# Column totals, spread of norms and transposition of three batches: from TensorE to VectorE's 32x32 blocks and DRAM

## Chip, cores and metric

The kernel runs on one core of a Trainium2 chip. The metric is the device time of one execution in microseconds. A core has five engines that work in parallel, each on its own list of instructions in order: PE (TensorE, matmuls, with PEld for its weight loads), DVE (VectorE), ACT (ScalarE), POOL (GpSimd) and SP (SyncE, which here issues the DMA transfers). Times of three runs before: 2155.27 us at the median, 2154.85 to 2155.99.

## What is computed

Channel attention for four batches, followed by a gated layer for all tokens. Cut to what matters:

```python
# q, k, v: (4, 6080, 256) float32; w_in (256, 2048), w_out (2048, 256)
qn = q / (norm(q, axis=1) + 1e-6)          # one norm per column, over 6080 rows
kn = k / (norm(k, axis=1) + 1e-6)
s  = kn.transpose(0, 2, 1) @ qn / tau      # 256 x 256 per batch
a  = softmax(s)
x  = (v @ a).reshape(24320, 256)
h  = x @ w_in
g  = h * sigmoid(1.702 * h)
out = g @ w_out
```

The weights come in and leave as 64-bit words of which the kernel uses 32-bit floats. Every large product is made of three products of high and low parts.

## The kernel before

**The main loop.** The product `v @ a @ w_in` is made as `v @ (a @ w_in)`: for each batch the 256x256 attention is folded into the input weights, and the main loop multiplies `v` by the folded weights. A step of the main loop is a *pair*: one batch, one chunk of tokens (six in a batch, of twice 512 tokens, one of twice 480) and two blocks of the hidden layer, eight pairs to a chunk. A pair issues 45 matmuls: 21 of `product` (line 800, seven products by a seven-product scheme in three terms, into the PSUM banks `ps_x`, `ps_y`, `ps_z`) and 24 of `project` (line 876, into `ps_o`). Between them stand ACT's copies and gates (`copied` line 834, `seed` 839, `gate` 854, `high` 859) and DVE's sums and low parts (`add` 843, which makes `r` from `ps_x`, and `low` 863, which makes `gl`). Results leave by `out_T` (line 891), issued by SP through three `osb` buffers.

**The side work.** While batch b is being multiplied, the attention of batch b + 1 is prepared in the gaps of the other engines: loads of q and k, their high and low parts, scores (`score_half`, line 388, gathered by `collect`, 406), and squares for the norms (ACT squares, POOL adds into `acc`, a tile of 128 partitions by 256 columns for q and for k). The rest is one chain per batch:

- `norms_sum` (415): four matmuls of `acc` with a column of ones give the sum over partitions of each column, `ps_n`; in float32 each matmul is two passes. `norms_copy` (424), `norms_root` on POOL (427), `norms_b` (431 to 436: plus 1e-6, reciprocal, and `diag`, the identity scaled by the norms of q).
- `norms_spread` (441): two matmuls of ones with `diag` put the norms of q in every partition, `ps_b`; `norms_q` (448) copies them to `rq`.
- `softmax_a` (495, 499), `softmax_b` (504, the exponential), `softmax_c` (517).
- `transposes` (525): four passes of PE turn the 256x256 attention `x` over, into `ps_t`. `turned` and `turned_low` (534, 537) make its parts `aT_h`, `aT_l`; `mixed` (546 on ACT copies `ps_t` to `whole`, 556 on DVE makes four sums of its quarters), and `mixed_split` (563, 565) their parts.
- `fold_load` (575) brings parts of the input weights from DRAM, `fold` (592) multiplies, and `fold_take` (603 on ACT for a first copy, 606 on DVE for a sum) puts the block product into `wf`. POOL and ACT and DVE make the weights of the next batch of it.

**What sets the order.** Each engine's instructions are put in one list by a planner that is written in the kernel: a `Job` is a row of steps with an engine, a planned duration, what each needs, a due time and an earliest begin, both counted in pairs. The planner places the steps in the gaps that it expects. PE's side work goes only into three slots of a pair (`at=("S", None)` is one of them). `turn` gives the step that must be over before a buffer may be used again. The first batch has a start-up of its own, written out by hand.

Of the kernel before, what the change touches and what calls it, by code (L numbers as in the profile page):

```python
# [11 lines left out]
F32 = mybir.dt.float32  # L12
# [3 lines left out]
ALU = mybir.AluOpType  # L16
AX = mybir.AxisListType
# [11 lines left out]
def channel_attention_then_glu(  # L29
# [169 lines left out]
    class Attention:  # L199
# [210 lines left out]

        def norms_sum(self):
            self.ps = bank("s", "ps_n")
            for n in range(2 * NC2):
                acc, i = self.acc[:, n // NC2, :], n % NC2
                nc.tensor.matmul(  # L415
                    self.ps[:, n : n + 1],
                    lhsT=acc[:, i * P : (i + 1) * P],
                    rhs=ones[:, 0:1],
                    start=True, stop=True,
                )  # L420

        def norms_copy(self):
            self.rn = small.tile([P, 2 * NC2], F32, tag="rn", name="rn")
            nc.vector.tensor_copy(self.rn, self.ps[:, : 2 * NC2])
# [4 lines left out]
        def norms_b(self):  # L429
            rn = self.rn  # L430
            nc.vector.tensor_scalar_add(rn, rn, 1e-6)
            nc.vector.reciprocal(rn, rn)
            self.diag = sp.tile([P, NC2, P], F32, tag="sq", name="diag", bufs=2)
            for i in range(NC2):
                nc.vector.tensor_scalar_mul(self.diag[:, i, :], ident, rn[:, i : i + 1])
            nc.vector.tensor_scalar_mul(rn[:, NC2:], rn[:, NC2:], rtau)

        def norms_spread(self):
            self.ps = bank("s", "ps_b")
            for i in range(NC2):  # L440
# [100 lines left out]
        def mixed(self, n):  # L541
            if n == 0:
                both = sp.tile([P, 2, NC2 * C], F32, tag="qs", name="mixed")
                self.whole = both[:, 0].rearrange("p (c x) -> p c x", c=NC2)
                self.mix = both[:, 1].rearrange("p (n x) -> p n x", n=4)
                nc.scalar.copy(self.whole, self.ps)
                return
# [7 lines left out]
            )[n - 1]  # L555
# [38 lines left out]
        def fold_take(self, s, k, n):  # L594
# [7 lines left out]
            if add is None:  # L602
                nc.scalar.copy(at[out], src)
# [863 lines left out]
    def weight_job(b, s, begin):  # L1467
# [9 lines left out]
        for k, (_, _, takes) in enumerate(FOLD):  # L1477
# [9 lines left out]
            for n, name in enumerate(names):  # L1487
                eng = "DVE" if k else "ACT"
                job.add(eng, 1.1, name, [(*key, k) if n == 0 else names[n - 1]], A.fold_take, s, k, n)
# [108 lines left out]
    def softmax_job(b, begin):  # L1598
        A = ats[b]
        job = Job(begin, begin)  # L1600
# [6 lines left out]
        last += [("sums", b, len(A.units))]  # L1607
        add("PE", 0.4, "sum", last, A.norms_sum, at=("S", None))
        add("DVE", 0.3, "copy", [(*key, "sum")], A.norms_copy)
        add("POOL", 1.0, "root", [(*key, "copy")], A.norms_root)  # L1610
        room = turn("sq", (*key, "b"), [(*key, "spread")])
        add("DVE", 2.4, "b", [(*key, "root"), *room], A.norms_b)
        add("PE", 0.6, "spread", [(*key, "b")], A.norms_spread, at=("S", None))
        room = turn("sq", (*key, "q"), [(*key, "x")])
        add("DVE", 0.6, "q", [(*key, "spread"), *room], A.norms_q)
        room = turn("qs", (*key, "x"), [(*key, "t")])
        add("DVE", 3.6, "x", [(*key, "q"), *room], A.softmax_a)
# [3 lines left out]
        add("PE", 0.7, "t", [(*key, "c")], A.transposes, at=("S", None))  # L1621
        add("ACT", 1.0, "turn", [(*key, "t")], A.turned)
        job.add("DVE", 1.15, ("turned", b), [(*key, "turn")], A.turned_low)
        room = turn("qs", (*key, ("mix", 0)), [("mixed", b)])
        add("ACT", 1.0, ("mix", 0), [("turned", b), *room], A.mixed, 0)
        for n in range(1, 5):
            add("DVE", 0.45, ("mix", n), [(*key, ("mix", n - 1))], A.mixed, n)
        used = [("fold", b, NG // 2 - 1, len(FOLD) - 2)]
        room = turn("sq", (*key, ("mix", "h")), used) + turn("sq", (*key, ("mix", "h")), used)
        add("ACT", 1.0, ("mix", "h"), [(*key, ("mix", 4)), *room], A.mixed_split, False)  # L1630
# [161 lines left out]
    for b in range(B):  # L1792
# [6 lines left out]
        if b + 1 < B:  # L1799
# [15 lines left out]
            softmax_job(b + 1, o + p + 1)  # L1815
# [44 lines left out]
```

## Time and profile before

| what | before |
|---|---|
| time, median of 3 runs | 2155.27 us (2154.85 to 2155.99) |
| time of the profiled execution | 2155.06 us |
| its span | 2153.1 us |
| mean granted clock of PE | 0.999 |
| busy PE / PEld / DVE / ACT / POOL | 100 / 83 / 61 / 72 / 20% |
| share of the chain that ended last: PE | 98% |
| matmuls on lines 876 (3 x 1536) and 800 (21 in each of 192 pairs) | 4608 and 4032 |
| share of the DMA engines used | 24% |

The span runs from the first to the last instruction that the profiler recorded; the 2 us that the execution takes longer lie around it. The records of matmuls overlap, so the busy share of PE is read with care: what a matmul takes of the stream is the distance between the starts of its neighbours. Idle time of the other engines costs nothing as long as PE doesn't wait for them.

### The profile page before, as it was taken

How to read it: one execution, taken by the hardware profiler on the slowest of the kernel's cores; microseconds unless marked ns; L12 is line 12 of the kernel's file. 1: busy time of each engine (PE TensorE's matmuls, PEld its weight loads, DVE VectorE, ACT ScalarE, POOL GpSimd, SP SyncE). 2: the span in 40 equal slices, each digit the busy share in tenths (PEclk: the TensorE clock that was granted, in tenths of full speed). 3: DMA queues.
4: the chain of work that ended last, by engine and by line, in shares of the span. 5: the costliest groups of instructions: out<-in, count | busy, mean ns of one | idle time of the engine just before them, and what ended most of it. 6: DMA issues, size and time to landing. Idle time of an engine off the chain costs nothing.

```text
span 2153.1 us, 26788 instructions
## 1 busy us (share of the span) xinstructions
PE 2144.7 (100%) x9702; PEld 1791.1 (83%) x9702; DVE 1321.3 (61%) x1990; ACT 1548.6 (72%) x2749; POOL 436.1 (20%) x465
## 2 busy tenths in 40 slices
PE   9999999999999999999999999999999999999999
PEld 8888888888888888888888888888888888888887
DVE  7986666665566666665566666666566555445543
ACT  7987777777667777776766777777676666666665
POOL 0003234330212323231021332332102110100100
PEclk9999999999999999999999999999999999999999
DMA  9433325221322222221122222132122110110100
GB/s 371 164 103 98 118 94 166 74 79 40 108 87 79 64 78 66 95 73 33 55 92 88 84 64 88 50 97 75 30 71 94 54 55 25 54 40 20 57 20 19
DMA packets 89397, 173.45 MB, mean 81 GB/s; under 512 B 8624, under 2 KB 16304, under 8 KB 89264
## 3 DMA queue, kind: packets, MB, share of 16 engines
q1 hardware_dynamic: 89264, 171.74, 24.0%
q8 instruction: 76, 1.25, 0.2%
q14 instruction: 57, 0.47, 0.1%
HBM read 136.32 MB, written 35.39 MB: 80 GB/s over the span
## 4 chain that ended last, share of the span: by engine, by line
PE 98%; ACT 1%; DMA 1%; DVE 0%; issue 0%; ACTq 0%; SPq 0%
PE ps_o L876 48%; PE ps_x L800 24%; PE ps_z L800 12%; PE ps_y L800 6%; PE s L388 4%; PE s L349 2%; PE ps_w L592 1%; DMA words<-in_w_in 1%; PE ps_w L645 0%; DMA words<-in_w_out 0%; PE ps_y L901 0%; ACT g L854 0%; ACT z L134 0%; DVE vl L782 0%; PE ps_n L415 0%
## 5 line engine op out<-in xcount | busy, mean ns | idle before, releaser
L876 PE MATMUL ps_o<-gh,wo_l 128*128 128x512 f32 (+1 forms) x1536 | 594.9, 387 | 0.0
L876 PE MATMUL ps_o<-gh,wo_h 128*128 128x512 f32 (+1 forms) x1536 | 594.8, 387 | 0.0
L876 PE MATMUL ps_o<-gl,wo_h 128*128 128x512 f32 (+1 forms) x1536 | 470.5, 387 | 0.0
L863 DVE TENSOR_TENSOR gl<-g,gh 128x512 fp32r<-128x512 f32 (+1 forms) x384 | 271.9, 747 | 147.3 <-ACT gh L859 147.2
L876 PEld LDWEIGHTS ps_o<-gh,wo_h 128*128 128x128 f32 x1536 | 288.3, 188 | 57.6
L876 PEld LDWEIGHTS ps_o<-gh,wo_l 128*128 128x128 f32 x1536 | 288.3, 188 | 57.5
L876 PEld LDWEIGHTS ps_o<-gl,wo_h 128*128 128x128 f32 x1536 | 288.3, 188 | 57.4
L333 POOL TENSOR_TENSOR acc<-acc,sq 128x256 f32<-128x256 f32 x276 | 216.2, 789 | 497.5 <-ACT sq L321 486.6
L863 DVE TENSOR_TENSOR gl<-ps_y,gh 128x512 fp32r<-128x512 f32 (+1 forms) x192 | 131.7, 686 | 291.2 <-ACT gh L859 290.7
L800 PE MATMUL ps_x<-vh,wh 128*128 128x512 f32 (+1 forms) x768 | 299.5, 390 | 0.7 <-ACT g L854 0.2
L800 PE MATMUL ps_x<-vl,wh 128*128 128x512 f32 (+1 forms) x768 | 298.1, 388 | 0.0
L800 PE MATMUL ps_x<-vh,wl 128*128 128x512 f32 (+1 forms) x768 | 297.5, 387 | 0.0
L765 POOL TENSOR_TENSOR v_raw<-v_raw 128x512 f32<-128x512 f32 (+1 forms) x110 | 160.9, 1471 | 622.3 <-DMA v_raw<-in_vT 525.3
L854 ACT ACTIVATE r<-r 128x512 f32<-128x512 f32 (+1 forms) x192 | 120.5, 628 | 174.8 <-DVE r L843 174.8
L834 ACT COPY r<-ps_x 128x512 f32<-128x512 f32 (+1 forms) x189 | 110.2, 583 | 165.8 <-PE ps_x L800 164.9
L859 ACT CAST gh<-g 128x512 fp32r<-128x512 f32 (+1 forms) x384 | 216.3, 613 | 0.1
L863 DVE TENSOR_TENSOR gl<-r,gh 128x512 fp32r<-128x512 f32 (+1 forms) x192 | 143.1, 745 | 62.4 <-ACT gh L859 59.4
L800 PEld LDWEIGHTS ps_x<-vh,wh 128*128 128x128 f32 x768 | 144.4, 188 | 29.6 <-ACT g L854 1.8
L800 PEld LDWEIGHTS ps_x<-vh,wl 128*128 128x128 f32 x768 | 144.2, 188 | 28.9
L834 ACT COPY r<-ps_z 128x512 f32<-128x512 f32 (+1 forms) x192 | 111.9, 583 | 77.4 <-PE ps_z L800 77.4
L800 PEld LDWEIGHTS ps_x<-vl,wh 128*128 128x128 f32 x768 | 144.5, 188 | 25.4
L406 DVE TENSOR_TENSOR sums<-sums,s 128x256 f32<-128x256 f32 x138 | 58.0, 420 | 158.0 <-PE s L388 155.6
(147 smaller groups left out, 3314.1 us busy)
## 6 DMA issues: line engine op xcount, KB each, us to landing
v_raw<-in_vT SPq DMA_DIRECT2D x80, 512.0 KB, 4.2
out_T<-osb SPq DMA_DIRECT2D x80, 256.0 KB, 2.0
raw_q<-in_q SPq DMA_DIRECT2D x74, 256.0 KB, 2.7
raw_k<-in_k SPq DMA_DIRECT2D x74, 256.0 KB, 2.7
fold<-t SPq DMA_DIRECT2D x48, 256.0 KB, 2.9
fold<-b SPq DMA_DIRECT2D x36, 256.0 KB, 2.9
v_raw<-in_vT SPq DMA_DIRECT2D x16, 480.0 KB, 3.8
words<-in_w_in SPq DMA_DIRECT2D x8, 512.0 KB, 5.3
```

The costliest lines, as they stand in the source:

```text
L333: nc.gpsimd.tensor_tensor(acc, acc, sq[:, j, :], op=ALU.add)
L349: nc.tensor.matmul(self.s[:, i, :], lhsT=lhsT, rhs=rhs, start=self.first, stop=last, skip_group_check=True,)
L388: nc.tensor.matmul(out, lhsT=ks[:, j, low, ci], rhs=rhs, start=n == 0, stop=n == len(terms) - 1, skip_group_check=True,)
L406: nc.vector.tensor_tensor(out, out, part, op=ALU.add)
L592: nc.tensor.matmul(self.ps, lhsT=l, rhs=r, start=n == 0, stop=n == 2)
L765: eng.tensor_tensor(out, a, z, op=ALU.subtract)
L800: nc.tensor.matmul(out, lhsT=l[:, wi, :], rhs=r[:, n, : self.hw], start=first and m == 0, stop=last and m == 2, skip_group_check=True,)
L834: nc.scalar.copy(r, getattr(self, src))
L854: nc.scalar.activation(g, source, AF.Gelu_apprx_sigmoid)
L859: nc.scalar.copy(gh, g)
L863: nc.vector.tensor_tensor(gl, g, gh.bitcast(F32), op=ALU.subtract)
L876: nc.tensor.matmul(out[d][:, : self.hw], lhsT=l[:, at_f, d * P : (d + 1) * P], rhs=r, start=first and l is wo[0] and r is gh, stop=last an ...
```

## The change

Batches 2 to 4 (`b` from 1 to 3 in the code) are touched; the first keeps its own start-up.

- **Column totals.** DVE transposes `acc` in blocks of 32x32 (`norms_blocks`) and sums each block's rows (`norms_part`, 128x512 to 128x16). The 128x16 part sums go to DRAM (`norms_out`) and come back by four loads whose innermost run is one number (`norms_in`, `quarters`, 32x16x1 four times), and a reduce of DVE gives `rn`.
- **Spread.** The norms of q go to a row in DRAM (`norms_q_out`) and come back to all partitions by one broadcast load into `rq` (`norms_q`). `diag` and PE's spread are gone.
- **Transposition.** DVE transposes `x` in 32x32 blocks (`turn_blocks`), eight stores put the blocks in their places in DRAM (`turn_out`, runs of 128 B), and one load brings the whole back (`turn_in`, `whole`). ACT's `mixed` copy is gone, since `whole` is now in SBUF.
- **Copies of block products.** `fold_take` makes its first copy on DVE, as it does the sums.
- **Planner.** `softmax_a` is two steps; the job of a batch begins one pair sooner and is due two pairs later; waits for the transfers are planned.

```diff
+        def norms_blocks(self):
+            self.blocks = sp.tile([P, 2 * C], F32, tag="sq", name="blocks", bufs=2)
+            nc.vector.transpose(self.blocks, self.acc.rearrange("p n c -> p (n c)"))
+        def norms_part(self):
+            self.part_sums = small.tile([P, 2 * C // 32], F32, tag="part", name="part")
+            nc.vector.tensor_reduce(
+                self.part_sums, self.blocks.rearrange("p (b v) -> p b v", v=32), axis=AX.X, op=ALU.add
+            )
+        def norms_out(self):
+            self.part_rows = dram.tile([P, 2 * C // 32], F32, name=f"part_rows{self.b}")
+            nc.sync.dma_start(self.part_rows, self.part_sums)
+        def norms_in(self):
+            self.quarters = small.tile([P, 2 * NC2, P // 32], F32, tag="quarters", name="quarters")
+            src = self.part_rows.rearrange("(a u) (n b) -> b u n a", u=32, b=P // 32)
+            for b in range(P // 32):
+                nc.sync.dma_start(self.quarters[32 * b : 32 * b + 32], src[b])
         def norms_sum(self):
-            self.ps = bank("s", "ps_n")
-            for n in range(2 * NC2):
-                acc, i = self.acc[:, n // NC2, :], n % NC2
-                nc.tensor.matmul(
...
             self.rn = small.tile([P, 2 * NC2], F32, tag="rn", name="rn")
-            nc.vector.tensor_copy(self.rn, self.ps[:, : 2 * NC2])
+            nc.vector.tensor_reduce(self.rn, self.quarters, axis=AX.X, op=ALU.add)
...
-            self.diag = sp.tile([P, NC2, P], F32, tag="sq", name="diag", bufs=2)
-            for i in range(NC2):
-                nc.vector.tensor_scalar_mul(self.diag[:, i, :], ident, rn[:, i : i + 1])
...
-        def norms_spread(self):
...
+        def norms_q_out(self):
+            self.q_row = dram.tile([1, C], F32, name=f"q_row{self.b}")
+            nc.sync.dma_start(self.q_row.rearrange("o (n p) -> p (o n)", p=P), self.rn[:, :NC2])
...
         def norms_q(self):
             self.rq = sp.tile([P, C], F32, tag="sq", name="rq", bufs=2)
-            nc.vector.tensor_copy(self.rq, self.ps[:, :C])
+            nc.sync.dma_start(self.rq, self.q_row[0].partition_broadcast(P))
...
+        def turn_blocks(self):
+            nc.vector.transpose(self.turned_x, self.x)
+        def turn_out(self):
+            self.turned_rows = dram.tile([C, NC2, P // 32, 32], F32, name=f"turned{self.b}")
+            to = self.turned_rows.rearrange("(n u) i a v -> a i u n v", u=32)
+            for a in range(P // 32):
+                for i in range(NC2):
+                    src = self.turned_x[32 * a : 32 * a + 32, i].rearrange("u (n v) -> u n v", v=32)
+                    nc.sync.dma_start(to[a, i], src)
+        def turn_in(self):
...
+            nc.sync.dma_start(
+                self.whole, self.turned_rows.rearrange("(j p) i a v -> p j (i a v)", p=P)
+            )
+            self.ps = self.whole
...
-                nc.scalar.copy(self.whole, self.ps)
...
             if add is None:
-                nc.scalar.copy(at[out], src)
+                nc.vector.tensor_copy(at[out], src)
...
-        job = Job(begin, begin)
+        job = Job(begin + 3, begin)
...
-            softmax_job(b + 1, o + p + 1)
+            softmax_job(b + 1, o + p)
```

How the lists of the engines stand before and after, at the three places of the chain. First PE in batch 2, where the column totals stood (`ps_n`, between the last products of one pair with `wo` and the first of the next with `wh`). Before:

```order
L876 MATMUL ps_o<-gh,wo_h 128x512
L876 MATMUL ps_o<-gh,wo_l 128x512
L876 MATMUL ps_o<-gl,wo_h 128x512 x2
L415 MATMUL ps_n<-ones,acc 128x1 x4
L800 MATMUL ps_x<-vh,wh 128x512
L800 MATMUL ps_x<-vl,wh 128x512
```

After, PE at the same place (line numbers are 18 higher):

```order
L894 MATMUL ps_o<-gh,wo_h 128x512
L894 MATMUL ps_o<-gh,wo_l 128x512
L894 MATMUL ps_o<-gl,wo_h 128x512 x2
L818 MATMUL ps_x<-vh,wh 128x512
L818 MATMUL ps_x<-vl,wh 128x512
L818 MATMUL ps_x<-vh,wl 128x512
```

The group has left the list and nothing of PE's has come in its place.

Second, DVE in batch 3, in the pair in which the totals come back. Before:

```order
L863 TENSOR_TENSOR gl<-r,gh 128x480
L863 TENSOR_TENSOR gl<-g,gh 128x480 x2
L406 TENSOR_TENSOR sums<-sums,s 128x256 x2
L782 TENSOR_TENSOR vl<-v_raw,vh 128x1024
L863 TENSOR_TENSOR gl<-ps_y,gh 128x480
L843 TENSOR_TENSOR r<-ps_x,r 128x480
L843 TENSOR_TENSOR ps_z<-ps_z,r 128x480
```

After, DVE at the same place:

```order
L881 TENSOR_TENSOR gl<-r,gh 128x480
L417 TENSOR_REDUCE part<-blocks 128x16
L881 TENSOR_TENSOR gl<-g,gh 128x480 x2
L406 TENSOR_TENSOR sums<-sums,s 128x256 x2
L800 TENSOR_TENSOR vl<-v_raw,vh 128x1024
L433 TENSOR_REDUCE rn<-quarters 128x4
L881 TENSOR_TENSOR gl<-ps_y,gh 128x480
L861 TENSOR_TENSOR r<-ps_x,r 128x480
L861 TENSOR_TENSOR ps_z<-ps_z,r 128x480
L440 TENSOR_SCALAR rn<-rn 128x4
```

The reduce of the block sums stands half a pair ahead of the reduce that waits for their return, and that one stands directly ahead of `gl<-ps_y` and `r<-ps_x,r`.

Third, SP in batch 3, with the transfers of all four steps (`part_rows`, `quarters`, `q_row`, `rq`, `turned`). Before:

```order
L891 DMA out_T<-osb 128x512 x4
L750 DMA v_raw<-in_vT 128x2x512 x2
L575 DMA fold<-b_0_426 128x512 x2
L575 DMA fold<-b_0_431 128x512 x2
L750 DMA v_raw<-in_vT 128x2x512 x2
L891 DMA out_T<-osb 128x480 x4
```

After, SP at the same place:

```order
L909 DMA out_T<-osb 128x512 x4
L768 DMA v_raw<-in_vT 128x2x512 x2
L423 DMA part_rows_9390<-part 128x16
L593 DMA fold<-b_0_426 128x512 x2
L429 DMA quarters<-part_rows_9390 32x16x1 x4
L593 DMA fold<-b_0_431 128x512 x2
L445 DMA q_row_9485<-rn 128x2x1
L452 DMA rq<-q_row_9485 128x256
L768 DMA v_raw<-in_vT 128x2x512 x2
L533 DMA turned_9714<-x 32x8x32 x8
L539 DMA mixed<-turned_9714 128x2x256
L909 DMA out_T<-osb 128x480 x4
```

Sixteen transfers have come between the loads of `v_raw` and `fold` and the stores of `out_T`, and each of them waits for an engine or for the transfer ahead of it.

## Rows read from the trace of the kernel before

**Rows 1.** The page: the span, and busy us, share of the span and instructions.

```profile
span 2153.1 us, 26788 instructions
PE 2144.7 (100%) x9702; PEld 1791.1 (83%) x9702; DVE 1321.3 (61%) x1990; ACT 1548.6 (72%) x2749; POOL 436.1 (20%) x465
```

**Rows 2.** Windows: length, busy us per engine, clock, DMA share, GB/s.

```profile
170.00:2150.00 1980.00, 1977.87 (x8933) 1653.60 (x8932) 1176.35 (x1734) 1405.78 (x2478) 431.97 (x453) 1.00 0.21 69
```

**Rows 3.** Timeline of PE, batch 2: start, us, engine, line, operation, shapes, count.

```profile
486.63 0.94 PE L415 MATMUL ps_n<-ones,acc 128*128 128x1 f32 x8
...
490.30 0.39 PE L800 MATMUL ps_x<-vh,wh 128*128 128x512 f32 x1
...
493.02 0.39 PE L800 MATMUL ps_x<-vh,wh 128*128 128x512 f32 x1
...
497.79 0.61 PE L441 MATMUL ps_b<-diag,ones 128*128 128x128 f32 x4
...
499.62 0.40 PE L876 MATMUL ps_o<-gh,wo_h 128*128 128x512 f32 x1
...
528.13 0.60 PE L525 MATMUL ps_t<-ident,x 128*128 128x128 f32 x4
...
529.88 0.37 PE L876 MATMUL ps_o<-gh,wo_h 128*128 128x480 f32 x1
```

**Rows 4.** Timeline of PE, batch 3, two neighbours six matmuls apart.

```profile
981.53 0.37 PE L800 MATMUL ps_z<-vh,wh 128*128 128x480 f32 x1
...
982.83 0.37 PE L876 MATMUL ps_o<-gh,wo_h 128*128 128x480 f32 x1
```

**Rows 5.** Groups by line and shape: busy us, mean ns, idle before.

```profile
L499 DVE TENSOR_REDUCE m<-x 128x1 f32<-128x256 f32 x8 | 3.4, 420 | 0.3
...
L606 DVE TENSOR_TENSOR wf<-wf,ps_w 128x512 f32<-128x512 f32 x42 | 28.8, 685 | 25.9 <-PE ps_w L592 25.8
...
L603 ACT COPY wf<-ps_w 128x512 f32<-128x512 f32 x6 | 3.5, 587 | 5.6 <-PE ps_w L592 5.6
```

**Rows 6.** Timeline of DVE, batch 3 (idle time before, and what ended it).

```profile
979.78 0.66 DVE L863 TENSOR_TENSOR gl<-r,gh 128x480 fp32r<-128x480 f32 x1
...
986.50 1.22 DVE L782 TENSOR_TENSOR vl<-v_raw,vh 128x1024 fp32r<-128x1024 f32 x1
988.18 0.66 DVE L863 TENSOR_TENSOR gl<-ps_y,gh 128x480 fp32r<-128x480 f32 x1 [0.47 <-ACT gh L859]
988.96 0.66 DVE L843 TENSOR_TENSOR r<-ps_x,r 128x480 f32<-128x480 f32 x1
...
996.16 0.87 DVE L406 TENSOR_TENSOR sums<-sums,s 128x256 f32<-128x256 f32 x2 [1.15 <-PE s L388]
...
1012.84 1.23 DVE L863 TENSOR_TENSOR gl<-g,gh 128x480 fp32r<-128x480 f32 x2 [1.07 <-ACT gh L859]
```

**Rows 7.** Timeline of PE's weight loads, batch 3: the load of `m4`.

```profile
990.50 0.19 PEld L800 LDWEIGHTS ps_x<-vh,wh 128*128 128x128 f32 x1
```

**Rows 8.** DMA: KB each and us to landing; one issuing line (min/median/max ns).

```profile
out_T<-osb SPq DMA_DIRECT2D x80, 256.0 KB, 2.0
...
raw_q<-in_q SPq DMA_DIRECT2D x3, 128.0 KB, 2.0
...
fold<-t SPq DMA_DIRECT2D x48, 256.0 KB, 2.9
...
L266 SPq DMA_DIRECT2D raw_q<-in_q x77: 327/340/720, 0.7 to 1474.5; - x77
```

**Rows 9.** DMA queue in the span, 4 to 24 us, and 40 to 60 us.

```profile
q1 hardware_dynamic: 89264, 171.74, 24.0%
...
q1 hardware_dynamic: 2310, 8.15, 101.8%
...
q1 hardware_dynamic: 3316, 7.89, 102.2%
```

**Rows 10.** Timeline of ACT, batch 3: the copy of `ps_x` in one pair.

```profile
1017.20 0.56 ACT L834 COPY r<-ps_x 128x480 f32<-128x480 f32 x1 [2.31 <-PE ps_x L800]
```

More of the change, by code (lines that the diff above doesn't have):

```diff
@@ L541, in mixed @@
         def mixed(self, n):
[L542 to L545, printed above, removed]
-                nc.scalar.copy(self.whole, self.ps)
-                return
             w, m = self.whole, self.mix
@@ L1487, in weight_job @@
             for n, name in enumerate(names):
-                eng = "DVE" if k else "ACT"
-                job.add(eng, 1.1, name, [(*key, k) if n == 0 else names[n - 1]], A.fold_take, s, k, n)
+                job.add("DVE", 1.1, name, [(*key, k) if n == 0 else names[n - 1]], A.fold_take, s, k, n)
         ends_at = [[(*key, "c", k, len(FOLD[k][2]) - 1)] for k in FOLD_ENDS]
@@ L1606, in softmax_job @@
         last = [summed[b, i] for i in range(2)]
[L1607 to L1613, printed above, removed]
+        room = turn("sq", (*key, "blocks"), [(*key, "part")])
+        add("DVE", 1.05, "blocks", [*last, *room], A.norms_blocks)
+        add("DVE", 1.05, "part", [(*key, "blocks")], A.norms_part)
+        job.add("SP", 0, (*key, "out"), [(*key, "part")], A.norms_out, wait=3.5)
+        job.add("SP", 0, (*key, "in"), [(*key, "out")], A.norms_in, wait=5.0)
+        add("DVE", 0.3, "sum", [(*key, "in")], A.norms_sum)
+        add("POOL", 1.5, "root", [(*key, "sum")], A.norms_root)
+        add("DVE", 0.6, "b", [(*key, "root")], A.norms_b)
+        job.add("SP", 0, (*key, "qo"), [(*key, "b")], A.norms_q_out, wait=3.5)
+        add("DVE", 0.3, "k", [(*key, "b")], A.norms_k)
         room = turn("sq", (*key, "q"), [(*key, "x")])
-        add("DVE", 0.6, "q", [(*key, "spread"), *room], A.norms_q)
-        room = turn("qs", (*key, "x"), [(*key, "t")])
-        add("DVE", 3.6, "x", [(*key, "q"), *room], A.softmax_a)
+        job.add("SP", 0, (*key, "q"), [(*key, "qo"), *room], A.norms_q, wait=3.5)
+        room = turn("qs", (*key, "x0"), [(*key, "out2")])
+        add("DVE", 1.6, "x0", [(*key, "q"), ("sums", b, len(A.units)), *room], A.softmax_a, 0)
+        add("DVE", 1.6, "x", [(*key, "x0")], A.softmax_a, 1)
         maker[*key, "exp"] = job
@@ L1620, in softmax_job @@
         add("DVE", 1.8, "c", [(*key, "exp")], A.softmax_c)
-        add("PE", 0.7, "t", [(*key, "c")], A.transposes, at=("S", None))
-        add("ACT", 1.0, "turn", [(*key, "t")], A.turned)
+        add("DVE", 1.05, "tblocks", [(*key, "c")], A.turn_blocks)
+        job.add("SP", 0, (*key, "out2"), [(*key, "tblocks")], A.turn_out, wait=5.0)
+        room = turn("qs", (*key, "whole"), [("mixed", b)])
+        job.add("SP", 0, (*key, "whole"), [(*key, "out2"), *room], A.turn_in, wait=4.0)
+        add("ACT", 1.0, "turn", [(*key, "whole")], A.turned)
         job.add("DVE", 1.15, ("turned", b), [(*key, "turn")], A.turned_low)
[L1624 to L1627, printed above, removed]
+        for n in range(4):
+            add("DVE", 0.45, ("mix", n), [(*key, ("mix", n - 1)) if n else ("turned", b)], A.mixed, n)
         used = [("fold", b, NG // 2 - 1, len(FOLD) - 2)]
         room = turn("sq", (*key, ("mix", "h")), used) + turn("sq", (*key, ("mix", "h")), used)
-        add("ACT", 1.0, ("mix", "h"), [(*key, ("mix", 4)), *room], A.mixed_split, False)
+        add("ACT", 1.0, ("mix", "h"), [(*key, ("mix", 3)), *room], A.mixed_split, False)
         job.add("DVE", 1.15, ("mixed", b), [(*key, ("mix", "h"))], A.mixed_split, True)
```

26 lines of the change are left out of this document (9 added, 17 removed).

## Prediction

> **What bounds the kernel now.** I read the page's busy shares first. TensorE (PE) is busy 2144.7 of 2153.1 us, VectorE (DVE) 61%, ScalarE (ACT) 72%, GpSimd (POOL) 20% [rows 1]. A share of 100% may still hide small gaps, since a matmul's record overlaps its neighbour's, so I then asked for the windows view behind the start-up: from 170 to 2150 us PE is idle for 2.1 of 1980 us [rows 2]. There PE is the bound, and every other engine is cover. So two questions decide: how many microseconds of PE work go, and whether something that replaces them makes PE wait at a place where it does not wait now.
>
> **What goes.** What a small matmul is worth is not its busy time but what it adds between the starts of its neighbours. The timeline of PE in batch 2 gives it [rows 3].
> - Column totals (eight passes of `ps_n`): two matmuls with twelve regular ones between their starts are 490.30 and 493.02, that is 2.72 us, or 0.227 each. With the same twelve plus the group it is 486.63 to 490.30, 3.67 us. The group costs 3.67 - 2.72 = 0.95.
> - Spread (four passes of `ps_b`): 497.79 to 499.62 is 1.83, with six regular matmuls in it (6 x 0.227 = 1.36): 0.47.
> - Transposition (four passes of `ps_t`): 528.13 to 529.88 is 1.75, with six matmuls of the 480-wide chunk. Six of those take 982.83 - 981.53 = 1.30 [rows 4]. It costs 0.45.
>
> That is 1.87 a batch. Batches 3 and 4 issue the same passes, so I take the same there: 3 x 1.87 = 5.6 us. Nothing else on PE goes; the score and fold matmuls only stand elsewhere among the regular ones.
>
> **What comes, DVE and ACT.** Per batch DVE gets two 32x32 block transposes of 128x512, one reduce of 128x512, one of 128x16, and two first copies of a block product (`wf`) from ACT; it loses `rn`'s copy, `diag` and `rq`'s copy. ACT loses the `mixed` copy and two `wf` copies. No block transpose is in this trace. The nearest row is an elementwise 128x512 of 0.685 us [rows 5]; half of it to twice it (0.35 to 1.4) are my bounds, and I take 0.69. A reduce of 128x256 takes 0.42 [rows 5]; for 128x512 I take 0.69 as well. The two copies go from 0.587 on ACT to 0.69. Together this is some 3.6 us of DVE a batch, of which about 1 is given back. DVE is idle 39% of the time, so I cost it at nothing, with two points to watch. First, DVE's `r<-ps_x,r` gates the last hidden matmuls of a pair. In batch 3 it runs from 988.96 to 989.62 [rows 6] and the weight load that waits for it starts at 990.50 [rows 7]: 0.88 us of cover. One extra instruction of 0.69 ahead of it still fits, two don't. Second, `wf` on DVE, a rival below.
>
> **What comes, the round trips.** Four chains now run over DRAM, each behind a wait of SyncE (SP), of DVE, or of both. As no transfer in pieces of 4 B shows in the trace, here is the real unknown. I work out the tightest place, the totals of batch 3.
> - DVE's `gl<-r` ends at 979.78 + 0.66 = 980.44 [rows 6]; the reduce `part` follows, to 981.1.
> - SP sends 128 rows of 64 B. A store of 128 rows lands in 2.0 at the median (256 KB), and so does the shortest load [rows 8]: 983.1. The `fold` loads beside it fall into this wait.
> - Four loads fetch 512 pieces of 4 B each. An issue takes SP 0.34 [rows 8], so the last is out by 983.1 + 4 x 0.34 = 984.5 and lands by 986.5 if a piece costs little. If a piece costs an engine p, 2048 pieces on 16 engines are 128p, and the landing is the later of 986.5 and 983.1 + 2.0 + 128p.
> - DVE's reduce to `rn` stands behind `vl` (to 987.72) and ahead of `gl<-ps_y` (988.18) and `r<-ps_x,r` [rows 6]. DVE stands still until the data lands, and then needs 0.2 (the reduce, an estimate for 16 elements a row, against 0.42 for 256) + 0.66 + 0.66 before 990.50, with 0.1 for the hand-over: the limit of the landing is 988.9, so p = 29 ns.
>
> What is p? Two stretches with full queues tell a little. 2310 packets and 8.15 MB took 101.8% of 16 engines in 20 us, that is 325.8 engine-us; 3316 packets and 7.89 MB took 327.0 [rows 9]. Solved for a price per packet and one per byte, this is 11 ns a packet. An upper bound is the mean of all packets, most of them of 2 KB: 24.0% x 16 x 2153.1 / 89264 = 92.6 ns [rows 9]. A 4 B piece carries almost no bytes, so I take 11 ns, with the landing at 986.5 and 2.4 us to spare. The stall is nothing, and the ends of its range are 0 and 8.1 us (92.6 ns: 985.1 + 11.9 = 997.0).
>
> A page of the Trainium skill speaks against this edit: "VectorE: DVE Perf Modes", section The three transpose paths, says that a plain DMA that transposes by strides is 19 times slower than the DMA's own transposing path, 1309 ns for 128x128. As an estimate from that page, 24.9 us x 16 / 16384 is 24 ns a piece; by it the landing would be 988.2, under the limit by 0.7: the sum would stay, but I would then give the first rival below 0.4. No run here shows it so far.
>
> The other chains have more room. The row `q_row` (256 pieces of 4 B, then a broadcast) is two landings behind `rn`, and its reader `softmax_a` comes after the last sums, which start at 996.16 [rows 6]: 990.8 + 4.0 = 994.8. For the transposition of batch 3, `gl<-g` ends at 1014.07 [rows 6], the blocks at 1014.8; eight stores of 256 runs of 128 B take SP 8 x 0.34 = 2.7 and land by 1019.5, and the load of 256 KB takes 2.9 as `fold` does [rows 8]: 1022.4. Its first reader is ACT's `aT_h`, just ahead of `r<-ps_x`. That copy ran at 1017.20 behind 2.31 us of idle time [rows 10]; it comes again one pair of 45 matmuls later (9.8), and 0.9 sooner as the totals have left that pair: 1026.1. Less 0.59 for the cast and 0.1, the data may land until 1025.4; 3.0 us to spare, p up to 44 ns. Behind SP's waits stand loads of `v_raw` and stores `out_T`; these are late by at most the waits' length, with three `osb` buffers and a chunk of lead, at nothing. POOL's `root` waits for `rn`, and `v_raw` sums behind it; POOL is 80% idle.
>
> **The sum.** The profiled execution took 2155.06 us. 2155.06 - 5.6 + 0 = 2149.5; the median stands 0.2 higher (2155.27), so I forecast **2149.7**. By the unsure sizes in it (pitch read to 0.05, nine groups) it is 2148.8 to 2150.8.
>
> **Rivals.** First: *the small pieces are dearer than the slack*. At 40 ns the totals land at 985.1 + 5.1 = 990.2, 1.3 late, and PE waits as long in each batch: +3.9, **2153.6**. For it speaks that nothing here prices such pieces, and that DVE really has nothing else to do meanwhile, as it works in order; against it, the 11 ns. This is no difference that can be measured: I call within 0.2% (4.3 us, about what a measurement of this kernel can tell from no change) the same. Second, the other side: *DVE's wait for the totals stops PE for longer than the gain*. At 92.6 ns each batch waits 8.1: 2149.7 + 24.3 = **2174**. It decides once the stalls exceed 5.6 + 4.3 = 9.9 us, 3.3 a batch, from 29 + 3300 / 128 = 55 ns. Against it speaks that the price is that of 2 KB packets. Third: *the first `wf` copies sit on the path*. The product's PSUM bank is free only once DVE has copied it, and DVE is then also due at `r<-ps_x,r`; were all six copies to show at 0.69, +4.1, **2153.8**. Against it: ACT's copies of 0.587 [rows 5] lay as near to their readers, and one such copy is inside the 0.88. That the change doesn't do what it says is out: in its order the PE groups of batches 2 to 4 are gone.
>
> **How the numbers follow.** Forecast 0.60; dear pieces 0.24; the DVE copies 0.06; slower by a long wait 0.10. The range for 8 in 10 must reach past the forecast's own 2148.8 to 2150.8 to the first and third rival, so 2148.8 to 2154. Faster is the forecast, 0.60; same are the two middle ones, 0.30; slower 0.10.
>
> **What would show it.** Right: three gaps of PE gone, no new idle time of PE, DVE's `rn<-quarters` waiting less than 1.2 us beyond 987.72's place, and the small loads landing in about 2 to 4 us. Wrong at the price of a piece: these loads take over 6 us to land, DVE's wait names a DMA, and PE waits for DVE's `r<-ps_x,r` right behind. Wrong at the transposition: ACT waits for `mixed` ahead of `r<-ps_x`. Wrong at the copies: PE's wait names `wf`. Wrong at the first step: the distance between neighbours of a removed group has not shrunk by 1.87 a batch.

## The result, and the profile after

| | before | after |
|---|---|---|
| time, median of 6 runs each | 2155.01 us (2154.55 to 2155.99) | 2172.67 us (2168.62 to 2173.61) |
| ratio, 95% interval | | 1.0079 (1.0066 to 1.0092) |
| time of the profiled execution | 2155.06 us | 2173.61 us |
| mean granted clock of PE | 0.999 | 0.994 |

The change made the kernel 17.7 us slower, where 5.6 us less were forecast (2155.27 to 2149.7). The page after, its span, busy shares and the chain that ended last:

```profile
span 2171.8 us, 26774 instructions
PE 2148.0 (99%) x9654; PEld 1791.5 (82%) x9654; DVE 1328.0 (61%) x1996; ACT 1543.3 (71%) x2740; POOL 439.0 (20%) x465
...
PE 94%; DMA 3%; ACT 1%; DVE 1%; issue 0%; SPq 0%; POOL 0%; DVEq 0%; ACTq 0%
PE ps_o L894 46%; PE ps_x L818 23%; PE ps_z L818 11%; PE ps_y L818 6%; PE s L388 4%; PE s L349 2%; PE ps_w L610 1%; DMA q_row<-rn 1%; DMA rq<-q_row 1%; DMA words<-in_w_in 0%; PE ps_w L663 0%; DMA part_rows<-part 0%; DVE gl L881 0%; DVE r L861 0%; DMA quarters<-part_rows 0%
```

Beside [rows 1], PE has 48 instructions fewer and is nevertheless busy for longer, and the share of PE in the chain has fallen from 98 to 94%. New in it are the transfers `q_row<-rn` and `rq<-q_row`, the two trips of the row of norms, with 1% each. The waits of PE name the place (engine and line, what it waited for, us in total, times, longest):

```profile
PE ps_x L818 <- DVE r L861: 15.9, 3, 6.8
...
PE ps_o L894 <- DVE gl L881: 0.8, 1, 0.8
```

Three waits, one in each of batches 2 to 4, for `r<-ps_x,r`: the very instruction of which the prediction said that it gates the last hidden matmuls of a pair. But it did not stand behind the column totals. The timeline of DVE in batch 3, to be read against [rows 6]:

```profile
992.61 0.16 DVE L433 TENSOR_REDUCE rn<-quarters 128x4 f32<-128x16 f32 x1
...
1001.14 0.88 DVE L406 TENSOR_TENSOR sums<-sums,s 128x256 f32<-128x256 f32 x2 [1.15 <-PE s L388]
1010.36 0.48 DVE L500 SCALAR_TENSOR_TENSOR x<-sums,rn,rq 128x256 f32<-128x256 f32 x1 [8.35 <-DMA rq<-q_row]
1010.88 0.42 DVE L504 TENSOR_REDUCE m<-x 128x1 f32<-128x256 f32 x1
1011.22 0.65 DVE L881 TENSOR_TENSOR gl<-ps_y,gh 128x480 fp32r<-128x480 f32 x1
1011.78 0.65 DVE L861 TENSOR_TENSOR r<-ps_x,r 128x480 f32<-128x480 f32 x1
```

The totals are back without a wait at 992.61. At 1002.0 DVE is through with the sums and comes to the first softmax step, which needs `rq`; it stands still for 8.35 us, and behind it, in order, stand `gl<-ps_y` and `r<-ps_x,r`, for which PE waits. On the timeline of SP the row's store, its broadcast, and the next load:

```profile
995.56 0.37 SPq L445 DMA_DIRECT2D q_row<-rn  x1
1003.91 0.32 SPq L452 DMA_DIRECT2D rq<-q_row  x1
1004.34 0.90 SPq L768 DMA_DIRECT2D v_raw<-in_vT  x2
```

SP may issue the broadcast only when the store has landed: 1003.91 - 995.56 = 8.35 us (that DVE's wait is 8.35 as well is chance). The broadcast then lands in another 6.4. The DMA rows of the page and of the trace (KB each, median us to landing), to be read against [rows 8]:

```profile
turned<-x SPq DMA_DIRECT2D x24, 32.0 KB, 1.6
mixed<-turned SPq DMA_DIRECT2D x3, 256.0 KB, 2.7
...
rq<-q_row SPq DMA_DIRECT2D x3, 128.0 KB, 6.4
...
quarters<-part_rows SPq DMA_DIRECT2D x12, 2.0 KB, 2.4
...
part_rows<-part SPq DMA_DIRECT2D x3, 8.0 KB, 2.2
q_row<-rn SPq DMA_DIRECT2D x3, 1.0 KB, 8.4
```

The smallest of all these transfers, 1 KB, is the slowest. The four loads in 4 B pieces, 2048 of them, are among the quick ones.

The idle time of PE is 15.9 + 0.8 = 16.7 us, and 5.6 of work have gone. That explains 11.1 of 18.5 us between the profiled executions. The rest is on the timeline of PE in batch 3 behind the wait:

```profile
1005.70 0.59 PE L894 MATMUL ps_o<-gl,wo_h 128*128 128x480 f32 x2
1012.48 0.77 PE L818 MATMUL ps_x<-vh,wh 128*128 128x480 f32 x1 [6.19 <-DVE r L861]
...
1017.05 0.58 PE L818 MATMUL ps_z<-vh,wl 128*128 128x480 f32 x1
1017.45 0.39 PE L818 MATMUL ps_x<-vh,wh 128*128 128x480 f32 x1
```

and in the windows of the same stretch (busy us of PE, PEld, DVE, ACT and POOL, then the granted clock):

```profile
1004.00:1006.00 2.00, 2.00 (x11) 1.65 (x9) 0.00 (x0) 0.00 (x0) 0.00 (x0) 1.00 0.00 0
1006.00:1008.00 2.00, 0.29 (x2) 0.00 (x0) 0.00 (x0) 0.00 (x0) 0.00 (x0) 1.00 0.09 29
...
1010.00:1012.00 2.00, 0.00 (x0) 0.00 (x0) 1.60 (x4) 0.00 (x0) 0.00 (x0) 0.66 0.87 337
1012.00:1014.00 2.00, 1.52 (x4) 1.32 (x5) 1.28 (x3) 1.51 (x3) 1.01 (x1) 0.50 0.03 11
...
1018.00:1020.00 2.00, 2.00 (x11) 1.74 (x10) 0.42 (x1) 1.89 (x3) 0.00 (x0) 1.00 0.00 0
```

While PE was idle its granted clock fell from 1.00 to 0.50, that is from the level of 2.4 to that of 1.2 GHz, and it came back only after PE had worked again for about 5 us. Twelve matmuls from 1012.48 to 1017.45 took 4.97 us and not 12 x 0.217 = 2.60 [rows 4]: 2.4 us more. Counted in the same way, the 14 slow matmuls behind the wait of batch 2 took 2.9 us more (each 0.227 before, as they are 512 wide) and the 14 of batch 4 2.7. So the books are 16.7 + 8.0 - 5.6 = 19.1 us against 18.5 measured between the profiled executions; with the 6.1 us that the runs without a stall gained below, in place of 5.6, they are 18.6.

### The profile page after: what moved, and what is told of

The parts are those of the page before. It is cut to its first block, busy times and chain, and to the rows that moved or that the text cites. A ratio compares the mean times of both kernels' runs of the same rounds, so it can differ in the third digit from the quotient of the medians.

```text
span 2171.8 us, 26774 instructions
## 1 busy us (share of the span) xinstructions
PE 2148.0 (99%) x9654; PEld 1791.5 (82%) x9654; DVE 1328.0 (61%) x1996; ACT 1543.3 (71%) x2740; POOL 439.0 (20%) x465
## 4 chain that ended last, share of the span: by engine, by line
PE 94%; DMA 3%; ACT 1%; DVE 1%; issue 0%; SPq 0%; POOL 0%; DVEq 0%; ACTq 0%
PE ps_o L894 46%; PE ps_x L818 23%; PE ps_z L818 11%; PE ps_y L818 6%; PE s L388 4%; PE s L349 2%; PE ps_w L610 1%; DMA q_row<-rn 1%; DMA rq<-q_row 1%; DMA words<-in_w_in 0%; PE ps_w L663 0%; DMA part_rows<-part 0%; DVE gl L881 0%; DVE r L861 0%; DMA quarters<-part_rows 0%
## 5 line engine op out<-in xcount | busy, mean ns | idle before, releaser
L818 PE MATMUL ps_x<-vh,wh 128*128 128x512 f32 (+1 forms) x768 | 300.4, 391 | 16.6 <-DVE r L861 15.9
L818 PEld LDWEIGHTS ps_x<-vh,wh 128*128 128x128 f32 x768 | 145.1, 189 | 47.1 <-DVE r L861 17.7
```

What stands on the lines that cost most here:

```text
L818: nc.tensor.matmul(out, lhsT=l[:, wi, :], rhs=r[:, n, : self.hw], start=first and m == 0, stop=last and m == 2, skip_group_check=True,)
```

## The experiments

**The theory** after this: the row's two trips take 14.8 us in place of the forecast's 4.0, DVE waits for them in order ahead of `r<-ps_x,r`, PE waits for DVE, and PE then runs for some microseconds at the lower clock. **Rivals**: the other trips through DRAM or DVE's added work cost as well; the place of the wait in DVE's list, not its length, is at fault.

**e2: the spread of norms on PE again, all else as changed.**

```diff
+            self.diag = sp.tile([P, NC2, P], F32, tag="sq", name="diag", bufs=2)
+            for i in range(NC2):
+                nc.vector.tensor_scalar_mul(self.diag[:, i, :], ident, rn[:, i : i + 1])
...
-            nc.sync.dma_start(self.rq, self.q_row[0].partition_broadcast(P))
+            nc.vector.tensor_copy(self.rq, self.ps[:, :C])      # ps: ones @ diag, on PE
```

> The change with its spread of norms undone: diag, two matmuls of ones and the copy to rq as before; column totals, transposition and copies of block products as in the change. Theory (only the row's two trips through DRAM cost): of the gain of 5.6 the spread's 1.4 are lost, nothing else is, and PE waits for nothing: 2155.0 - 4.2 = 2150.8 (2150 to 2152.5). Rival (the totals' and the transposition's trips, or DVE's added work, cost as well): PE shows waits for DVE or ACT in batches 2 to 4, and the time is 2154 or more.

Measured 2150.25 us (10 runs, 2149.61 to 2151.11), ratio 0.9978 (0.9968 to 0.9988). With before at 2154.86 in these runs that is 4.6 less, where 4.2 were expected, and no wait of PE is left that names a transfer or an instruction of DVE's in batches 2 to 4. So the totals' trip, the transposition's trip and DVE's added copies cost nothing that can be seen, and the parts that they replace are gained. The loss lies in the spread alone.

**e3: the column totals on PE again, row and transposition through DRAM.**

```diff
-        add("DVE", 1.05, "blocks", [*last, *room], A.norms_blocks)
...
+        last += [("sums", b, len(A.units))]
+        add("PE", 0.4, "sum", last, A.norms_sum, at=("S", None))     # four matmuls of acc with ones
+        add("DVE", 0.3, "copy", [(*key, "sum")], A.norms_copy)
```

> The change with its column totals undone: four matmuls of acc with ones and the copy to rn, after the last sums, as before; the row of norms still goes through DRAM, and so does the transposition. Theory: DVE still waits for rq, 8 us a batch, and PE behind it; the totals' 0.95 a batch come back on PE. The time is 2168 to 2180. Rival (the totals' trip is what sets the stall): without it the stall goes, and the time is 2155 less 2.8 (spread and transposition off PE), 2152 to 2155.

Measured 2179.23 us (4 runs, 2179.01 to 2181.37), ratio 1.0115 (1.0100 to 1.0130). DVE's wait for `rq` in the three batches together is 27.0 us, beside 25.4 in the changed kernel: it does not need the totals' trip. It is also slower than the change itself, though PE waits less for DVE (10.7 us in place of 16.7): the totals' 0.95 us a batch are back on PE, the chain now begins behind the last sums, and PE also waits 4.3 us for the high and low parts of the next batch's weights.

**e1: the planner is told the true lengths of the two trips.**

```diff
-        job.add("SP", 0, (*key, "qo"), [(*key, "b")], A.norms_q_out, wait=3.5)
+        job.add("SP", 0, (*key, "qo"), [(*key, "b")], A.norms_q_out, wait=13.0)
...
-        job.add("SP", 0, (*key, "q"), [(*key, "qo"), *room], A.norms_q, wait=3.5)
+        job.add("SP", 0, (*key, "q"), [(*key, "qo"), *room], A.norms_q, wait=10.0)
```

> The change with one edit: the planner is told that the store of the row of norms and its broadcast take 13 and 10 of its units (8.8 and 6.8 us) in place of 3.5 and 3.5 (2.4 us each); in the changed kernel's trace they landed in 8.4 and 6.4 us. So DVE's first softmax step stands about one pair later in its list. Theory (DVE waits in order for that row, PE behind it, and PE then runs at the lower clock): DVE's wait for rq falls from 25.4 us in all to under 3, PE's wait for DVE's r from 15.9 to under 1, the mean clock returns to 0.999, and the time is 2149.5 (2148.8 to 2152). Rival (the chain to the next batch's weights is too long to be moved): the wait for rq goes as well, but PE waits at the first pair of a batch for its weights, and the time stays above 2156.

Measured 2160.24 us (10 runs, 2157.14 to 2162.5), ratio 1.0023 (1.0014 to 1.0033): the rival's number, not mine. DVE's wait for `rq` fell from 25.4 to 3.3 us, about as both had it, but PE's waits are now these:

```profile
PE ps_z L818 <- DVE wl L702: 2.6, 2, 1.9
PE ps_x L818 <- ACT ps_y L857: 2.1, 2, 1.9
PE ps_z L818 <- ACT wh L704: 1.7, 2, 0.9
```

`wh` and `wl` are the high and low parts of the next batch's weights, the end of the chain. All but 0.2 us of these waits lie in the first pairs of batch 2, from 587 to 650 us, and behind them the granted clock falls to 0.61 in windows of 4 us. For batch 2 the longer plan brings the weights too late, for batches 3 and 4 it does not. So the long trip can't simply be planned for at its full length here; e10 below plans for a part of it.

**e4 and e8: what such transfers take by themselves.** Both are the kernel before with stores and loads added in its last batch, where SP has little to do.

> The kernel before with eleven small stores and eight loads added to the last batch, where SP has little to do, none of them read by anything: 256 pieces of 4 B side by side into a row of 1 KB (as the row of norms is stored), 256 pieces of 4 B each 64 B apart, 128 pieces of 8 B side by side, 8 runs of 128 B; then broadcast loads of 1 KB to 128 partitions from rows stored some 60 us or 10 us before. Theory A (neighbours in one short row are written one after another): the 4 B pieces side by side land in 7 to 9 us, 64 B apart in 2 to 3, 8 B in 4 to 5, the runs of 128 B in 2. Rival B (any store of 4 B pieces is slow): 64 B apart also takes 7 to 9 us. Theory C (128 readers of one row are slow): every broadcast lands in about 6.4 us. Rival D (a load is slow only right behind the store it waits for): the late broadcasts land in 2 to 2.5 us. The time stays at 2155, as no engine waits for any of it.

Measured 2156.17 us (one run). The 256 pieces of 4 B side by side landed in 8.5 to 11.5 us, 128 pieces of 8 B in 4.8 to 5.4; 8 runs of 128 B were over in 1.8, read from the load that waited for the last of them. The one store with pieces 64 B apart whose landing shows took 11.1 us and seemed to speak for rival B. But SP had issued it 0.7 us behind a store of pieces side by side, so both were in the DMA engines together. The question stayed open. Of the broadcasts the six whose landing shows took 2.9 to 5.2 us, neither theory C's 6.4 nor rival D's 2 to 2.5; the quickest was issued 1.8 us behind the store of its row. The next probe held each of its own transfers back until the one ahead of it was over:

```python
src = ones[:, : 2 * size].rearrange("p (n k) -> p n k", k=size)     # size numbers in a piece
nc.sync.dma_start(out.rearrange("n p k -> p n k"), src)             # 256 pieces side by side
nc.sync.dma_start(seen[0][0:1, :size], out[0, 0:1])                 # holds SP until they have landed
```

> The kernel before with a row of transfers in its last batch that nothing reads, one after another (behind each store a tiny load of it holds SP until it has landed): stores of 256 pieces of 4, 8, 16, 32, 64, 128 and 512 B side by side, stores of 256 pieces of 4 B that lie 64 B and 512 B apart, and loads of 128 KB, once 128 times the same 1 KB and once 128 rows of their own. Theory A (pieces that share a short stretch of DRAM are written one after another): 4 B side by side takes 8 us and 4 B at 64 or 512 B apart 2 to 3. Theory B (a piece below some size costs a DMA engine about 0.5 us wherever it lies; 256 pieces are 16 an engine): 4 B takes 8 to 9 us in all three places, and the price falls with the size, to 2 at 64 or 128 B. For the loads, theory C (many readers of one row are slow): 128 times the same 1 KB takes 4 or more, 128 rows 2.1; rival D (it was slow in the change because v_raw is issued right behind it): both take 2 to 2.5. The time is that of before but for what SP is held up.

Measured 2154.45 us (one run). The timeline of SP, each store and the load that waited for it:

```profile
1677.68 0.81 SPq L575 DMA_DIRECT2D fold<-b  x2
1678.55 0.73 SPq L907 DMA_DIRECT2D near_one<-ones  x1
1689.02 0.30 SPq L908 DMA_DIRECT2D seen<-near_one  x1
1689.37 0.39 SPq L911 DMA_DIRECT2D apart_line<-ones  x1
1690.98 0.23 SPq L912 DMA_DIRECT2D seen<-apart_line  x1
1691.27 0.37 SPq L911 DMA_DIRECT2D apart_row<-ones  x1
1692.88 0.23 SPq L912 DMA_DIRECT2D seen<-apart_row  x1
...
1749.45 0.97 SPq L750 DMA_DIRECT2D v_raw<-in_vT  x2
1750.47 0.46 SPq L907 DMA_DIRECT2D near_four<-ones  x1
1755.55 0.26 SPq L908 DMA_DIRECT2D seen<-near_four  x1
1755.86 0.37 SPq L907 DMA_DIRECT2D near_eight<-ones  x1
1757.44 0.24 SPq L908 DMA_DIRECT2D seen<-near_eight  x1
...
1994.26 2.05 SPq L750 DMA_DIRECT2D v_raw<-in_vT  x2
1996.36 0.46 SPq L916 DMA_DIRECT2D seen<-near_row  x1
2000.68 0.34 SPq L918 DMA_DIRECT2D seen<-near_row  x1
2002.74 0.32 SPq L916 DMA_DIRECT2D seen<-near_row  x1
```

The load behind a store is issued once the store has landed. The table gives the trace's own time to landing, which lies 0.1 us under the distance between the two starts (in the first `near_one` 0.9 under it). All stores are of 256 pieces, and each was made twice:

| pieces | us to landing |
|---|---|
| 4 B side by side (`near_one`), at first beside loads of the kernel | 9.6, 10.1 |
| 8 B side by side | 4.2, 3.2 |
| 16 B side by side (`near_four`), beside loads of `v_raw` | 5.1, 4.7 |
| 32 B side by side (`near_eight`) | 1.5, 1.5 |
| 64 B side by side | 1.5, 1.5 |
| 128 B side by side | 1.5, 1.6 |
| 512 B side by side | 1.8, 1.7 |
| 4 B, 64 B apart (`apart_line`) | 1.6, 2.0 |
| 4 B, 512 B apart (`apart_row`) | 1.5, 1.5 |

Theory A holds and B falls: a piece of 4 B is as cheap as any as long as it has 64 B of DRAM to itself. It is the many small writes into one short stretch that take long. The probe held back its own transfers, though, and not the kernel's: `near_one` and `near_four` were always issued right behind loads of `v_raw` or `fold`. While the first `near_four` was under way, the 16 engines were over 80% busy until 1754.5 and 3% behind that, so that its price can't be told from theirs. For 4 B the change itself is the cleaner row: in batch 3 the engines were at most 7% busy in any 2 us between 994 and 1004, and the store took 8.3. The 8 B stores had the engines to themselves as well, with 3.2 and 4.2, and so did those of 32 B. So the price falls somewhere between 4 and 32 B a piece, and where is not shown. Whether the engines or the memory put the writes one behind the other is not seen. The Trainium skill, "DMA: Bandwidth & Descriptors", section Specifications, has read-modify-write for transfers below 512 B; no run here shows a price that begins there, as 32 to 128 B landed sooner than 512.

Of the loads of 128 KB (line 916: 128 times the same 1 KB; line 918: 128 rows of their own) the first took 2000.68 - 1996.36 = 4.3 us, right behind loads of `v_raw`, the second 2.1. In the other turns the one row took 2.9 to 3.7, rows of their own 2.0 to 2.1. So C holds in direction, with about 1 us, but not for the whole 6.4 us that the broadcast took in the change.

**e5: the row in 8 runs of 128 B.** DVE multiplies 32 columns of ones with each half of the norms and transposes that in 32x32 blocks, so that 32 numbers lie side by side on one partition.

```diff
+            wide = sp.tile([P, 2, NC2, 32], F32, tag="sq", name="wide", bufs=2)
+            for n in range(NC2):
+                nc.vector.tensor_scalar_mul(wide[:, 0, n, :], ones[:, :32], rn[:, n : n + 1])
+            self.lying = wide[:, 1]
+            nc.vector.transpose(self.lying, wide[:, 0])
...
-            nc.sync.dma_start(self.q_row.rearrange("o (n p) -> p (o n)", p=P), self.rn[:, :NC2])
+            to = self.q_row.rearrange("o (n a u) -> (o a) n u", n=NC2, u=32)
+            nc.sync.dma_start(to, self.lying[0:P:32])
```

> The change with one edit: the norms of q are spread over 32 columns by DVE (two small multiplications of ones) and transposed in 32x32 blocks, so that the row goes to DRAM in 8 runs of 128 B and not in 256 pieces of 4 B; the broadcast load, the planner's waits and all else as in the change. In the probe a store of 8 such runs was over in 1.8 us, where 256 pieces of 4 B took 8.5 to 11.5. Theory (the store of 4 B pieces is the long part): the store lands in 2, the row is complete 1.7 + 6.4 = 8 us after its issue, DVE waits about 2 us a batch and PE up to 1: 2150 to 2153. Rival (the broadcast is slow because it reads what has just been written, however it was written): the load grows, and the stall stays above 3 us a batch: 2160 or more.

Measured 2148.95 us (7 runs, 2148.52 to 2149.51), ratio 0.9973 (0.9962 to 0.9983). That lies under the 2150 to 2153 of the theory, which had taken the broadcast at 6.4. It was issued 1.7 to 1.8 us behind the store in all three batches, and DVE doesn't wait for `rq`. In batch 2 no load of `v_raw` followed it for 8 us, and it landed in 3.0; in batches 3 and 4 one followed within 0.5 us, and it landed in 4.3 and 4.4. So rival D seems to have a part of the price, some 1.3 us. Behind a store in pieces of 4 B the same load took 5.9 to 6.4 in the change, with `v_raw` behind it, and 3.8 to 6.2 where no load followed (e3, and batches 3 and 4 of e1): what the rest of its price hangs on is open.

**e6: in addition no row is read by all partitions** (edit against e5).

```diff
-            to = self.q_row.rearrange("o (n a u) -> (o a) n u", n=NC2, u=32)
-            nc.sync.dma_start(to, self.lying[0:P:32])
+            nc.sync.dma_start(self.q_rows, self.lying)          # 128 rows of 256 B
...
-            nc.sync.dma_start(self.rq, self.q_row[0].partition_broadcast(P))
+            src = self.q_rows.rearrange("(a v) n u -> v n a u", v=32)
+            for c in range(P // 32):
+                to = self.rq[32 * c : 32 * c + 32].rearrange("v (n a u) -> v n a u", n=NC2, u=32)
+                nc.sync.dma_start(to, src)
```

> As the run with 8 runs of 128 B, but the whole 128x64 transposed tile goes to DRAM in one store of 128 rows of 256 B, and four loads fetch it to 32 partitions each, in runs of 128 B, so that no row of DRAM is read by all 128 partitions. Theory (the 4 B store and the broadcast are the stall, nothing else): store 2.2, four issues 1.8, landing 2.4, that is 6.4 us in place of 14.8, inside the 8.3 us that batch 3 had between the store's issue and the point from which PE waits. No wait of PE, the clock at 0.999, and the gain of all three parts: 2155.0 - 5.6 = 2149.4 (2148.5 to 2151). Rival (four more issues on SP and some 0.6 us of DVE in the chain use up the slack): PE waits 1 to 2 us in batches 3 and 4: 2152 to 2155.

Measured 2148.59 us (6 runs, 2147.29 to 2148.84), ratio 0.9969 (0.9957 to 0.9982), as expected. Store 1.4 us, the four loads 2.1 to 2.4 each.

In e5 and e6 the planner, told of the longer step on DVE, had also put the first softmax step up to half a pair later. So length and place had changed together, and the last two runs part them.

**e9: the short trip of e6 in the order of the change.** The planner's numbers for the step are left as in the change (edit against e6); DVE's list is then the changed kernel's, entry by entry, with the three small instructions added.

```diff
-        room = turn("sq", (*key, "b"), [(*key, "qo")])
-        add("DVE", 1.5, "b", [(*key, "root"), *room], A.norms_b)
+        add("DVE", 0.6, "b", [(*key, "root")], A.norms_b)
```

> The kernel with one store of 128 rows of 256 B and four loads, with the planner's numbers for that step left as in the change, so that DVE's list is the changed kernel's, entry by entry, but for the three small instructions that prepare the store. In the two runs with a short trip so far the planner had also moved the first softmax step later, by up to half a pair, which may have hidden a wait by itself. Theory (the trip's length is the cause): also in the old order DVE waits under 1.5 us a batch for rq, PE not at all: 2148.5 to 2150.5. Rival (the later place was the cause): DVE waits as long as in the change, 2160 or more.

Measured 2148.16 us (7 runs, 2147.24 to 2149.49), ratio 0.9972 (0.9961 to 0.9983). The timeline of DVE in batch 3, at the place where the change stood still for 8.35 us:

```profile
993.79 0.88 DVE L406 TENSOR_TENSOR sums<-sums,s 128x256 f32<-128x256 f32 x2 [1.16 <-PE s L388]
994.71 0.49 DVE L508 SCALAR_TENSOR_TENSOR x<-sums,rn,rq 128x256 f32<-128x256 f32 x1
995.23 0.42 DVE L512 TENSOR_REDUCE m<-x 128x1 f32<-128x256 f32 x1
996.27 0.66 DVE L889 TENSOR_TENSOR gl<-ps_y,gh 128x480 fp32r<-128x480 f32 x1 [0.62 <-ACT gh L885]
```

DVE's waits for `rq` are 1.8 us in all, the longest 1.4, and none of PE's names DVE in batches 2 to 4. The shorter trip is enough by itself. Store and broadcast were shortened together here. By an estimate from the rows of batch 3, e5's trip with the old broadcast behind a short store would just fit too: 995.56 + 1.7 + 4.3 = 1001.6, where DVE comes to the step at 1002.0. No run has it in this order.

**e10: the long trip at the later place.**

```diff
-        job.add("SP", 0, (*key, "qo"), [(*key, "b")], A.norms_q_out, wait=3.5)
+        job.add("SP", 0, (*key, "qo"), [(*key, "b")], A.norms_q_out, wait=7.5)
```

> The other half of that: the row stored in 256 pieces of 4 B and broadcast as in the change, but the planner is told 7.5 units (5.1 us) for the store and not 3.5, which moves DVE's first softmax step of batch 3 behind gl<-ps_y, the two sums and gl<-r, as in the runs with the short trip. Theory (length): the row lands 14.8 us after the store's issue, the step now stands some 5 us later, so DVE still waits 3 to 4 us in batches 3 and 4, PE 1 to 4, and the clock falls again: 2155 to 2166. Rival (place): no wait, 2148.5 to 2150.5.

Measured 2152.69 us (10 runs, 2150.86 to 2154.79), ratio 0.9992 (0.9982 to 1.0001): neither number. The theory had the waits of DVE right and what they cost wrong. Of the three waits for `rq`, 11.9 us together, this is the one in batch 3 on DVE's timeline, and under it is the only wait that is left of PE for DVE, in batch 2:

```profile
1002.67 0.66 DVE L881 TENSOR_TENSOR gl<-r,gh 128x480 fp32r<-128x480 f32 x1 [0.64 <-ACT gh L877]
1006.46 0.48 DVE L500 SCALAR_TENSOR_TENSOR x<-sums,rn,rq 128x256 f32<-128x256 f32 x1 [3.13 <-DMA rq<-q_row]
...
PE ps_x L818 <- DVE r L861: 1.9, 1, 1.9
```

In batches 3 and 4 the step now stands behind `r<-ps_x,r`, the sum for `ps_z` and `gl<-r`. There PE needs nothing of DVE for some microseconds, and waits of 3.1 and 4.0 us are free. In batch 2, where the step moved only behind two `gl<-g` and still stands ahead of `r<-ps_x,r`, DVE waits 4.8 us and PE 1.9, and the clock fell to 0.50 behind that. So what a wait costs is its length less the time until somebody needs the next entry of that list; to shorten the trip (e9) and to move the step past `r` (e10, batches 3 and 4) both take the stall away.

## Why the prediction was wrong

- **What goes from PE: right.** In e6 and e9, which keep all that the change removes and have no stall, the time is 6.1 us under before (2148.59 against 2154.66, 2148.16 against 2154.28), in e5 5.7; the sum had 5.6. The part without the spread was forecast as 5.6 - 1.4 = 4.2 and measured as 4.6.
- **DVE's and ACT's added work at nothing: right.** The block transposes took 0.70 us each and the reduce 0.68, where 0.69 was taken for each; the first copies of `wf` took 0.69. In no run with the short trip or without the row did a wait of PE name them. The rival of the `wf` copies falls.

```profile
L621 DVE COPY wf<-ps_w 128x512 f32<-128x512 f32 x6 | 4.2, 692 | 8.8 <-PE ps_w L610 8.8
...
L525 DVE STREAM_TRANSPOSE x<-x 128x512 f32<-128x512 f32 x3 | 2.1, 706 | 0.0
...
L417 DVE TENSOR_REDUCE part<-blocks 128x16 f32<-128x512 f32 x3 | 2.0, 682 | 0.0
```

- **The totals' trip: right in what counts.** I took this for the tightest place and for the unknown. Its four loads, 2048 pieces of 4 B, landed in 2.2 to 3.3 us each; DVE did not stand still for them in batch 3 and for 0.8 us in batch 4, and PE for none of it. A term was mis-sized: SP took 0.61 to 0.67 us for the issue of such a load, not 0.34. From the first issue to the last landing it was 4.3 to 4.4 us a batch, with 3.4 forecast, and the three later issues make up the difference. The prediction's estimate from the Trainium skill, "VectorE: DVE Perf Modes", section The three transpose paths, has 5.1 for that stretch and is not borne out; the page ties its 19 times to a large innermost stride of the destination, and here it is the source that has it.
- **The transposition's trip: right.** Stores 1.6 us, load 2.7, no wait of ACT for a transfer of it. SP took 3.8 us for the eight issues and not 2.7.
- **The row of norms: this is the step that failed.** The prediction put it down as "two landings behind `rn`", 990.8 + 4.0 = 994.8, and gave it more room than the totals. It took 8.35 + 6.4 = 14.8 us, in place of 4.0. The room was about right: by the prediction's rows the last sums end at 996.16 + 0.87 = 997.0, 6.2 us behind `rn`, and in the changed kernel DVE came to the step 6.4 us behind the store's issue. So DVE stood still for the rest of the trip, 8.35 us, with `r<-ps_x,r` behind it. Three things were passed over. The sum has no price of a piece for this store at all, only a plain landing. What lies beside what was not looked at: the 256 pieces of this store share 1 KB of DRAM, while the 2048 pieces of the totals are read, and 4 B side by side took 8.3 us here, against 1.5 to 2.0 for 4 B with 64 or 512 B between them in e8. And 128 readers of one row were given the landing of a load of 128 rows, 2.0, where e8 has 2.9 to 4.3. The row had no bounds, so its price was in no end of the range.
- **The rival on the slower side had the mechanism and missed the place.** It let DVE stand still 8.1 us a batch in its order and PE behind it, and came to 2174; DVE stood 8.35 in batch 3 and the time is 2172.67. That they agree is luck: the wait was for another transfer, with another cause, PE idled 16.7 us and not 24.3, and the difference was made up by the clock.
- **The clock was in no term.** Of the loss, 8 us are matmuls at the lower level behind the three waits, half as much as the idle time itself, on top of it.

## What to carry to other kernels

Where a step leaves a fully busy engine for a trip through DRAM, bound every transfer of the trip from both sides, the smallest too, and look at where its pieces lie, not only at how many bytes they are. A wait in an in-order list costs its length less the time until the next entry is needed, so look which entries stand behind it before believing in a busy share of 61%. And where the bound engine is TensorE, a wait of several microseconds costs more than it lasts: here 16.7 us of idle time drew 8 us of slow matmuls behind them, and the 1.9 us in e10 drew 1.7.

## What the runs showed of the hardware

- 256 writes of 4 B side by side into 1 KB of DRAM took 7.9 to 9.5 us in the change, e1, e3 and e10, and 9.6 and 10.1 in e8 behind large loads; the same 64 B or 512 B apart 1.5 to 2.0; 256 writes of 32 B side by side 1.5. Four loads of 512 pieces of 4 B each landed in 2.2 to 3.3 us each.
- A load that brings the same 1 KB to 128 partitions took 2.9 to 3.0 us with little else under way and 4.3 to 4.4 with loads of `v_raw` beside it (e5, e8), up to 6.5 behind a store in pieces of 4 B (e10), 128 rows of their own 2.0 to 2.1.
- PE's granted clock fell to 0.50, the level of 1.2 GHz, with idle times of 3.0 (behind one of 0.75), 6.2 and 6.8 us, and was back at 1.00 after 5 to 6 us of work at the lower level; in e10 it fell with an idle time of 1.9 us and was back after 4.
- A version with the short trip (e9, 0.9972, 0.9961 to 0.9983, and e6, 0.9969, 0.9957 to 0.9982) beats both the kernel before and the changed one.
